# Gate and value in seven products of halves, attention jobs on a fixed plan, and a norm over all lanes

## The chip, the cores and the metric

The kernel runs on one core of a Trainium2 chip. Its time is the device time of one execution in microseconds (us); each figure is a median of several runs. The engines are called PE (matrix products; PEld is its weight load), DVE (VectorE), ACT (ScalarE) and POOL (GpSimd). SBUF is the on-chip memory that tiles lie in, its rows are called partitions; PSUM is the set of banks that PE writes its products to.

## The reference

A retention block feeds a SwiGLU block. All of the first is fp32; three of the weights are float64 in memory and are converted to fp32 on the chip.

```python
scores = (1 / sqrt(64)) * q @ k.T             # 8 batches, 8 heads, 576 tokens, 64 wide
ret = scores * gamma[h] ** (i - j)            # for i >= j, else 0
x = (ret @ v)                                 # to 4608 tokens x 512
rms = sqrt(mean(x * x, -1) + 1e-6)
xn = x / rms * rms_g
g, val = xn @ w_gate, xn @ w_val              # 512 x 1536 each
out = (g * sigmoid(g) * val) @ w_out          # 1536 x 512
```

## The kernel before

Attention is done in 32 jobs, one for each batch and pair of heads. Each works in chunks of 128 tokens and carries a state from chunk to chunk. The second block works in 12 units of 384 tokens, with features on the partitions and tokens along the columns. A unit's gate and value products are called its up phase; three output blocks of 128 tokens follow. The parts that matter here are the norm, the gate product, and the loop that decides what comes next.

```python
def norm_1(u, sq):                       # sq: squares summed over the four feature blocks
    ms = bank(f"ms_{u}")
    for s in range(NS):                  # 3 blocks of 128 tokens; tokens go to the partitions
        nc.tensor.matmul(ms[:, s : s + 1], lhsT=sq[:, 0, s * P : s * P + P], rhs=mean_w, ...)
    nc.vector.tensor_scalar(out=r, in0=ms[:, :NS], scalar1=EPS, ..., op0=ALU.add)
    nc.gpsimd.tensor_tensor(out=r, in0=r, in1=mhalf.to_broadcast([P, NS]), op=ALU.pow)   # 3 columns
    for s in range(NS):
        nc.vector.tensor_scalar(out=diag[:, s], in0=ident, scalar1=r[:, s : s + 1], ..., op0=ALU.mult)

def norm_2(u, diag):                     # ones x diag: each token's factor on all partitions
    nc.tensor.matmul(rb[:, :U], lhsT=ones, rhs=diag..., start=True, stop=True)
    for c in range(NHP):
        nc.vector.scalar_tensor_tensor(out=x[:, c], in0=x[:, c], scalar=rms_g[:, c : c + 1],
                                       in1=rb[:, :U], op0=ALU.mult, op1=ALU.mult)

def project(u, f, w, ps):                # one of 12 row blocks of gate or value
    for c in range(NHP):
        nc.tensor.matmul(ps[:, :U], lhsT=w[:, c, f * P : f * P + P], rhs=x_of[u][:, c], ...)

# (cut) the main loop: products go on until attention lags, then attention_step() runs,
# often several times in a row
due = did_a == n_attn or (did_a / n_attn - LAG) * ffn_cols > did_f * (1 - LAG)
```

## Time and profile before

| | before |
|---|---|
| time | 1504.72 us (1502.89 to 1507.06) |
| PE busy / DVE busy / POOL busy | 1336 / 390 / 176 us |
| mean clock granted to PE | 0.933 |
| first gate product | 121.4 us |
| pow on POOL | 12 times 0.87 us, over 3 columns |

An engine's busy time counts overlapping instructions once. Each digit of the page's second part is the busy share of one fortieth of the span, in tenths. The prediction below shows those lines and reads them. The one row on pow (shortest, median and longest in ns, then first and last start, and its shape):

```profile
L284 POOL TENSOR_TENSOR r<-r,mhalf x12: 850/873/878, 98.7 to 1324.3; 128x3 f32<-128x3 f32 x12
```

### The profile page before, as it was taken

What the parts mean: (1) busy time and instruction counts of PE and PEld (TensorE: products, weight loads), DVE (VectorE), ACT (ScalarE), POOL (GpSimd) and SP (SyncE); (2) the same over time, 40 slices, a digit from 0 to 9 for tenths busy, and PEclk for the clock granted to TensorE, in tenths of its full rate; (3) what the DMA queues carried; (4) which work ended last, traced back from release to release, by engine and by line L of the source; (5) the groups of instructions that cost most, each with busy time, mean ns of one, the idle gap of its engine ahead of it and who ended that gap; (6) DMA issues with size and microseconds to landing.
All of it is one profiled execution on the core that took longest, in us unless ns stands there. A gap on an engine that the chain in (4) does not pass through costs nothing.

```text
span 1503.9 us, 13309 instructions
## 1 busy us (share of the span) xinstructions
PE 1335.9 (89%) x5312; PEld 777.0 (52%) x5312; DVE 390.4 (26%) x772; ACT 160.8 (11%) x310; POOL 175.9 (12%) x212
## 2 busy tenths in 40 slices
PE   2557896999999995699999996599999999699999
PEld 2554451555655545555554554465455554455554
DVE  4786878011122114320010112431010011220010
ACT  1112221001110101110000001010000000110000
POOL 3541000011111013400000012410000000200000
PEclk9668995999999997899999998789999999699999
DMA  8664333012121025400000014520000001000000
GB/s 167 141 147 91 112 104 106 22 38 45 31 45 38 0 45 110 82 1 9 13 0 21 0 38 89 100 41 0 21 0 8 14 0 36 1 0 7 14 0 21
DMA packets 244493, 66.22 MB, mean 44 GB/s; under 512 B 225744, under 2 KB 238160, under 8 KB 244432
## 3 DMA queue, kind: packets, MB, share of 16 engines
q1 hardware_dynamic: 228928, 46.17, 14.8%
q10 hardware_dynamic: 15504, 19.21, 4.1%
q8 instruction: 42, 0.69, 0.2%
q14 instruction: 19, 0.16, 0.0%
HBM read 55.91 MB, written 9.44 MB: 43 GB/s over the span
## 4 chain that ended last, share of the span: by engine, by line
PE 83%; DVE 9%; POOL 4%; DMA 2%; issue 1%; ACT 0%; ACTq 0%; SPq 0%; DVEq 0%; POOLq 0%
PE gate L307 24%; PE val L307 24%; PE out L331 24%; PE s L174 4%; PE av L225 3%; POOL sd L212 2%; DVE ret L196 2%; PE s L184 2%; POOL qT L144 2%; DVE sum L206 1%; DVE exp L475 1%; DMA v<-in_v_dram 1%; DVE exp L472 1%; DVE exp L449 1%; DVE w_out L478 0%
## 5 line engine op out<-in xcount | busy, mean ns | idle before, releaser
L307 PE MATMUL gate<-x,w_gate 128*128 128x384 f32 x1152 | 403.7, 494 | 18.4 <-DVE x L300 17.2
L307 PE MATMUL val<-x,w_val 128*128 128x384 f32 x1152 | 397.8, 489 | 3.5 <-ACT silu L317 3.0
L331 PE MATMUL out<-w_out,h 128*128 128x512 f32 x864 | 385.5, 605 | 13.8 <-DVE w_out L478 13.8
L307 PEld LDWEIGHTS gate<-x,w_gate 128*128 128x128 f32 x1152 | 221.2, 193 | 177.0 <-issue 27.6
L307 PEld LDWEIGHTS val<-x,w_val 128*128 128x128 f32 x1152 | 219.9, 191 | 157.9 <-ACT silu L317 3.7
L331 PEld LDWEIGHTS out<-w_out,h 128*128 128x128 f32 x864 | 165.1, 193 | 225.8 <-issue 194.6
L323 DVE TENSOR_TENSOR h<-silu,val 128x384 f32<-128x384 f32 x144 | 79.8, 554 | 738.7 <-PE val L307 736.7
L212 POOL TENSOR_SCALAR sd<-sum,gc 64x256 f32<-64x256 f32 x64 | 59.9, 937 | 1007.1 <-DVE sum L206 1004.2
L174 PE MATMUL s<-qT,kT 64*128 64x128 f32 (+1 forms) x640 | 68.9, 373 | 120.5 <-POOL qT L144 104.5
L317 ACT ACTIVATE silu<-gate 128x384 f32<-128x384 f32 x144 | 70.7, 492 | 611.8 <-PE gate L307 598.7
L174 PEld LDWEIGHTS s<-qT,kT 64*128 64x128 f32 (+1 forms) x640 | 57.3, 261 | 136.6 <-POOL qT L144 107.2
L196 DVE TENSOR_TENSOR ret<-s,causal 128x768 f32<-128x768 f32 (+2 forms) x96 | 47.4, 549 | 251.8 <-PE av L225 249.3
L337 ACT COPY o<-out 128x512 f32<-128x512 f32 x36 | 21.1, 587 | 364.9 <-PE out L331 364.9
L144 POOL TENSOR_TENSOR qT<-qT,gq 128x512 f32<-128x512 f32 x64 | 54.9, 877 | 13.3 <-DVE qT L139 10.8
L225 PE MATMUL av<-ret,v 128*64 128x128 f32 (+1 forms) x640 | 54.0, 318 | 0.1
L150 POOL TENSOR_TENSOR v<-v,gv 128x512 f32<-128x512 f32 x64 | 50.4, 807 | 3.5 <-DMA v<-in_v_dram 3.5
L249 ACT COPY x<-av 128x192 f32<-128x192 f32 (+1 forms) x80 | 23.6, 357 | 238.7 <-PE av L238 231.9
L225 PEld LDWEIGHTS av<-ret,v 128*64 128x64 f32 (+1 forms) x640 | 45.3, 172 | 6.9 <-issue 6.9
L238 PE MATMUL av<-qT,sd 128*128 128x128 f32 (+1 forms) x256 | 37.1, 290 | 2.2 <-POOL sd L212 2.2
L453 ACT ACTIVATE exp<-exp,least 128x512 f32<-128x512 uint32 x36 | 26.1, 724 | 111.2 <-DVE exp L449 111.2
L238 PEld LDWEIGHTS av<-qT,sd 128*128 128x128 f32 x256 | 32.7, 200 | 4.8 <-POOL sd L212 2.3
L184 PE MATMUL s<-v,k 128*64 128x64 f32 x512 | 31.4, 291 | 0.1
(40 smaller groups left out, 372.6 us busy)
## 6 DMA issues: line engine op xcount, KB each, us to landing
qraw<-in_q_dram SPq DMA_DIRECT2D x128, 72.0 KB, 2.4
kraw<-in_k_dram SPq DMA_DIRECT2D x128, 72.0 KB, 2.5
out_dram<-o SPq DMA_DIRECT2D x36, 256.0 KB, 2.0
k<-in_k_dram SPq DMA_DIRECT2D x64, 128.0 KB, 2.5
v<-in_v_dram SPq DMA_DIRECT2D x64, 128.0 KB, 2.7
w<-in_moe_w_gate_dram ACTq DMA_DIRECT2D x12, 512.0 KB, 3.7
w<-in_moe_w_val_dram ACTq DMA_DIRECT2D x12, 512.0 KB, 4.0
w<-in_moe_w_out_dram ACTq DMA_DIRECT2D x12, 512.0 KB, 3.5
```

The lines of the kernel that those rows point to most:

```text
L144: nc.gpsimd.tensor_tensor(out=t, in0=t, in1=gq[:, hp, :n].unsqueeze(1).to_broadcast([P, m, n]), op=ALU.mult)
L150: nc.gpsimd.tensor_tensor(out=t, in0=t, in1=gv[:n, hp].unsqueeze(1).unsqueeze(3).to_broadcast([n, m, 2, D]), op=ALU.mult,)
L174: nc.tensor.matmul(d["s"][blk][:n, e, o : o + n], lhsT=d["kT"][r, ck], rhs=d["qT"][r, ck], start=True, stop=True,)
L184: nc.tensor.matmul(d["s"][1][e * D : e * D + D, 0, SC + c * D : SC + c * D + D], lhsT=d["k"][:, c, e], rhs=d["v"][:, c, e], start=True, st ...
L196: nc.vector.tensor_tensor(out=ret[:n, :, c0 * P : c0 * P + m * n].rearrange("p e (c k) -> p e c k", c=m), in0=s[blk][:n, :, o : o + m * n] ...
L212: nc.gpsimd.tensor_scalar(out=sd[j % 2][r, :, r], in0=t[r], scalar1=gc[r, hp : hp + 1], scalar2=None, op0=ALU.mult,)
L225: nc.tensor.matmul(av[blk][e * D : e * D + D, o : o + n], lhsT=d["v"][:n, c, e], rhs=d["ret"][:n, e, c * P : c * P + n], start=(c in (0, A ...
L238: nc.tensor.matmul(av[blk][:, o : o + n], lhsT=sd[j % 2][:, c - 1], rhs=d["qT"][:, c * P : c * P + n], start=False, stop=(c in (AC - 1, NC ...
L307: nc.tensor.matmul(ps[:, :U], lhsT=w[:, c, f * P : f * P + P], rhs=x_of[u][:, c], start=(c == 0), stop=(c == NHP - 1),)
L317: nc.scalar.activation(out=h_of[u, f], in_=ps[:, :U], func=AF.Silu)
L323: nc.vector.tensor_tensor(out=h, in0=h_of[u, f], in1=ps[:, :U], op=ALU.mult)
L331: nc.tensor.matmul(ps[s][:, :DM], lhsT=h_of[u, f][:, s * P : s * P + P], rhs=w_out[:, f], start=(f == 0), stop=(f == NF - 1),)
```

## The change

Its intent is fewer products: with each matrix cut in two by two blocks, Winograd's form of Strassen's scheme needs seven products of halves where the plain one needs eight, at the price of additions on DVE. Attention jobs get fixed places among the products. Work is moved off POOL, and the norm is computed for all partitions at once, so that no diagonal matrix is needed. The diff is cut to its core.

```diff
 def norm_1(u):
-    for s in range(NS):
-        nc.tensor.matmul(ms[:, s : s + 1], lhsT=sq[:, 0, s * P : s * P + P], rhs=mean_w, ...)
-    nc.vector.tensor_scalar(out=r, in0=ms[:, :NS], ..., op0=ALU.add)
-    nc.gpsimd.tensor_tensor(out=r, in0=r, in1=mhalf.to_broadcast([P, NS]), op=ALU.pow)
-    (cut: the diagonal, and its product with ones)
+    nc.tensor.matmul(ms[:, :U], lhsT=ones, rhs=t_of[u], start=True, stop=True)   # ones = 1/512
+    nc.vector.tensor_scalar(out=r, in0=ms[:, :U], ..., op0=ALU.add)
+    nc.gpsimd.tensor_tensor(out=r, in0=r, in1=mhalf.to_broadcast([P, U]), op=ALU.pow)
 (cut)
+def up(u, m, g):                      # m: gate or value; two row blocks of each half
+    product(A11, x_, True);   nc.scalar.copy(out=s1, in_=pairs_of(x_))
+    product(S2, y, True);     add(u2, s1, y)
+    product(S1, z, True);     add(u4, u2, z)
+    product(A12, x_, False);  result(f, 0, "c11", None, x_)
+    product(S3, w, True);     result(f + NH, 1, "c22", u4, w)
+    product(S4, z, False);    result(f, 1, "c12", u2, z)
+    product(A22, w, False);   result(f + NH, 0, "c21", u2, w)
 (cut: in norm_2, four sums of x on DVE; in join, four sums of weights on POOL)
-        nc.gpsimd.tensor_tensor(out=t, in0=t, in1=gq[...], op=ALU.mult)        # t: qT
+            nc.vector.tensor_tensor(out=x_of[u][...], in0=av[blk][...], in1=gq[...], op=ALU.mult)
 (cut: the scaling of v and of the state from POOL to ACT; the clamp of exponents from DVE to ACT)
+SLOTS = (((0, 2, 4, 5), 5), ((6,), 9), ((1, 3, 5), 10))   # places of jobs in units 3k, 3k+1, 3k+2
+def behind(u, i):
+    at, n = SLOTS[u % 3]
+    if i in at:
+        slot(u // 3 * 8 + n + at.index(i))
+    if u + 1 < NU and 5 <= i < 8:                          # 5: last products; 6, 7: output blocks
+        (norm_0, norm_1, norm_2)[i - 5](u + 1)
```

## The prediction

> **What bounds the kernel now.** I read the page's first two parts, then its costliest groups, then a table by stage, then the waits of TensorE (PE).
>
> ```profile
> span 1503.9 us, 13309 instructions
> PE 1335.9 (89%) x5312; PEld 777.0 (52%) x5312; DVE 390.4 (26%) x772; ACT 160.8 (11%) x310; POOL 175.9 (12%) x212
> ...
> PE   2557896999999995699999996599999999699999
> ...
> DVE  4786878011122114320010112431010011220010
> ...
> PEclk9668995999999997899999998789999999699999
> DMA  8664333012121025400000014520000001000000
> ```
>
> PE is busy 89% of the span. It is thin only in the first seven slices (37.6 us each), where DVE stands at 4 to 8 tenths, and in three dips later.
>
> ```profile
> L307 PE MATMUL gate<-x,w_gate 128*128 128x384 f32 x1152 | 403.7, 494 | 18.4 <-DVE x L300 17.2
> L307 PE MATMUL val<-x,w_val 128*128 128x384 f32 x1152 | 397.8, 489 | 3.5 <-ACT silu L317 3.0
> L331 PE MATMUL out<-w_out,h 128*128 128x512 f32 x864 | 385.5, 605 | 13.8 <-DVE w_out L478 13.8
> L323 DVE TENSOR_TENSOR h<-silu,val 128x384 f32<-128x384 f32 x144 | 79.8, 554 | 738.7 <-PE val L307 736.7
> ```
>
> An fp32 product appears as two instructions (576 gate products, 1152 rows). The mean durations overlap; the pace comes from the chain of waits:
>
> ```profile
> 722.94 2.58 PE gate L307 x8
> 784.86 30.90 PE out L331 x72
> ```
>
> Eight instructions of 384 columns take 2.58 us, 322.5 ns each; 72 of 512 take 30.90, 429.2 each. Both are 2 x columns / 2.4 + 2.5 ns. At that pace the work is gate and value 2304 x 0.3225 = 743 us, output 864 x 0.4292 = 371, 32 attention jobs x 4.2 = 134 (one warm job runs from 912.71 to 916.91), norm about 16: 1264 us. The other 240 us of the 1504 are idle time and half clock. Where, by stage:
>
> ```profile
> 0.00:121.45 121.45, 55.92 (x557) 48.59 (x557) 86.72 (x150) 16.91 (x33) 59.02 (x67) 0.77 0.72 149
> 121.45:284.00 162.55, 144.08 (x377) 74.07 (x378) 104.34 (x202) 31.80 (x49) 1.73 (x2) 0.88 0.30 92
> ...
> 912.00:992.00 80.00, 48.22 (x467) 40.07 (x466) 32.22 (x73) 7.12 (x19) 34.44 (x43) 0.74 0.54 103
> 992.00:1054.00 62.00, 62.00 (x202) 37.09 (x201) 14.95 (x31) 8.65 (x14) 1.72 (x2) 1.00 0.01 2
> ```
>
> The columns are length, then busy time of PE, PEld, DVE, ACT, POOL, then clock, DMA share, GB/s. No gate product runs before 121 us, where nine attention jobs and the conversion of float64 weights share DVE. Later, whenever attention jobs come in a burst (912 to 992), a job takes 11 us for 4.2 us of PE work, because
>
> ```profile
> PE s L174 <- POOL qT L144: 104.5, 21, 5.8
> ```
>
> GpSimd scales the state and then q between one job and the next.
>
> **What the Trainium skill says.** "TensorE: Matmul & The Clock Gate", section "Back-to-back issue gap", gives N/2.4 + 2.5 ns warm; the trace agrees if each fp32 instruction counts its columns twice. Its section "LDWEIGHTS" gives P/1.2, 107 ns for 128 columns; in the trace the carried-state products with 128 columns start 111 to 112 ns apart, and so do the mean products with one column, so about 112 ns is the floor for a stream in which each product loads new weights. "VectorE: DVE Perf Modes", section on the errata, gives (N+151)/0.96 for an fp32 tensor_tensor: 557 ns at 384; the trace has 554. "GPSIMD Engine Reference", section 3.1, puts a two-input operation at about 2.6 cycles per element; the trace's 512-column multiplies take 1103 and 1297 ns. No page gives the cost of a pow there.
>
> **The change, part by part.**
>
> *Seven products.* Per unit of 384 tokens and matrix: 7 products x 6 row blocks x 2 halves = 84 matmuls of 192 columns in place of 48 of 384. One instruction should take 2 x 192 / 2.4 + 2.5 = 162.5 ns, above the 112 ns floor, so weight loading stays hidden. 12 units x 2 x 84 x 2 = 4032 instructions x 0.1625 = 655 us, 88 less than 743. The price is on DVE: per pair of gate row blocks 5 additions out of PSUM, per pair of value blocks 5 plus 4 multiplies, 14 x 36 = 504 operations x 0.554 = 279 us in place of 80. Within a unit's up phase (336 x 0.1625 = 54.6 us of PE) that is 42 x 0.554, some 23 to 25 us: it fits. The tightest wait is the last product, which accumulates on a bank that the addition before must have read: PE has one product, 8 x 0.1625 = 1.3 us, to cover it, and DVE needs 0.27 (in the trace, end of stream to start of h) + 0.55 + about 0.1. It fits if DVE's queue is empty.
>
> *Norm.* One broadcast mean product replaces three small ones and one diagonal product: 8 us less on PE. But pow on GpSimd goes from 3 columns to 384. Three took 873 ns; a GpSimd multiply extrapolated to zero width (458 ns at 64, 1297 at 512) is 338 ns. At most 535 / 3 = 178 ns per column remain, which would be 68 us per unit; if most of it is fixed, 10 to 20 us. This is the largest unknown. Between the mean product and the next unit's first product lie two output blocks, 20.6 us, less about 4 us for DVE: pow is hidden up to some 17 us. I take 20 us at the start, where nothing hides it, and hidden afterwards.
>
> *Attention.* q's decay moves into the copy out of PSUM, v's and the state's scaling to ACT. PE no longer waits for GpSimd to finish qT, and jobs are spread singly behind products instead of in bursts. DVE per job, from the rows by form: mask about 1.4, state sum 1.05, three copies of 192 columns 1.07, transposes 1.5, 5.0 us in all, beside 4.2 us of PE work and followed by products that need DVE late. So a job should cost its 4.2 us and perhaps 1 more.
>
> *Weights.* One DVE pass (0.496 us) of six goes to ACT: 3.9 down to about 3.4 us per chunk of 36. The four sums per group are GpSimd's: about 5 us x 6, beside other work.
>
> *Sum.* Start: the first transpose comes at about 15 us as now; five jobs x 5.0 plus eight chunks x 3.4 plus two chunks begun make 54 us of DVE; norm about 9 and pow 20: the first product at about 102 us (now 121.5, after nine jobs). Unit 0's up phase carries 28 chunks (95 us of DVE), its own 24 us and four jobs (20 us): 139 us of DVE against 72 of PE. With imperfect overlap 160. Then 11 up phases x 54.6 = 601, 12 down phases x 30.9 = 371, norms 8, the 24 jobs left x 4.2 = 101, tail 4, waits 25 (1 us per job). 102 + 160 + 601 + 371 + 8 + 101 + 4 + 25 = 1372; I say 1375.
>
> **The rivals.** (a) *Pow becomes the bound.* For it: 873 ns for three columns, no figure anywhere for more, and the state's scaling has been moved off GpSimd as if to keep it free. Against it: tiny instructions are mostly fixed cost, and the norm is split into three stages with an output block between. At 40 us per unit, 23 us of each would show: about 1375 + 20 + 11 x 23 = 1650; at 68 us about 1960. I give "visibly not hidden" one chance in five. (b) *DVE becomes the bound in steady state*, through its in-order queue: a job's 5 us burst ahead of the additions makes the last product of the next pair wait. For it: DVE rises from 390 to some 640 us. Against it: 45% of the span, and the first need after a job comes 2.6 us into the next pair. Two to three us per job and one per pair would add 100 to 120 us: about 1490, near the same. (c) *Half-width matmuls lose the gain*: if the pace were 190 ns (the recorded length of a weight load) instead of 162.5, gate and value would take 766 us and the change would keep only its scheduling part: about 1480. Against it: the 112 ns floor. (d) *The weight stage hides less*: unit 0 at half clock, since PE is busy only half of it; the trace shows clock 0.5 from 233 to 264 us in the same stage. That is 30 us more at most.
>
> **Range and chances.** If pow is hidden, waits of 0 to 100 us and a start of 85 to 140 us give about 1320 to 1450. The top of the range also takes a pow of about 28 us or a moderate form of (b). Range 1315 to 1500. Below 1473 (2% faster): 0.78. Within 2%: 0.07. Slower than 1534: 0.15, nearly all from (a).
>
> **What would show it.** The product rows of 192 columns should number 4032 and run 8 in 1.30 us. The pow row is the first to look at: over 17 us, DVE's scaling of x waits for it and PE for DVE at every unit's start. PE should wait for GpSimd nowhere in attention. The first product should come near 102 us, and the first output block near 262. DVE should be busy about 640 us and be PE's main releaser only in the first 260. It would be wrong if pow is long, if the waits of PE on DVE after unit 0 exceed 60 us, or if the 192-column pace is not 162.5.

## The result, and the profile after

| | before | after |
|---|---|---|
| time | 1504.72 us | 1877.23 us (1874.94 to 1879.2) |
| ratio | 1 | 1.2474 (95% interval 1.2449 to 1.2499) |
| PE / DVE / POOL busy | 1336 / 390 / 176 us | 1229 / 605 / 773 us |
| mean clock | 0.933 | 0.832 |
| first gate product | 121.4 us | 144.9 us |

The change makes the kernel a quarter slower. The page of the changed kernel:

```profile
span 1872.9 us, 17016 instructions
PE 1228.9 (66%) x6968; PEld 979.0 (52%) x6968; DVE 605.4 (32%) x1185; ACT 298.2 (16%) x570; POOL 772.5 (41%) x42
...
PE   3207657396397399198199099199099189379199
...
POOL 0492306607506604805704802902902901923900
PEclk9657878698699699599599599699599699789599
```

PE's busy time fell as planned. But PE now has a hole every few slices, and after the first slice POOL is busy wherever PE has its hole. Only 42 instructions ran on POOL in all. Twelve of them are the costliest group on the page, and under it stand two of the new products (columns: count, busy us, mean ns of one, then idle time ahead of the group and who ended it):

```profile
L301 POOL TENSOR_TENSOR r<-r,mhalf 128x384 f32<-128x384 f32 x12 | 738.2, 61519 | 873.5 <-DVE r L300 873.5
L336 PE MATMUL x<-x,w_gate 128*128 128x192 f32 x576 | 127.1, 371 | 551.4 <-DVE x L307 537.6
...
L336 PE MATMUL w<-sums,w_val 128*128 128x192 f32 x576 | 110.9, 338 | 12.1 <-DVE c L343 12.1
```

One pow takes 61.5 us. The products of the first kind begin each unit, and have 551 us of idle time ahead of them; those of the second kind, with the tight wait of the prediction, have 12. The table of waits gives the same chain from its two ends (total us, times, longest):

```profile
DVE x L307 <- POOL r L301: 740.4, 12, 61.7
...
PE x L336 <- DVE x L307: 537.6, 12, 63.0
```

DVE waits for pow, PE waits for DVE. In order of time, for the second unit of the changed kernel (start, length):

```profile
294.42 0.81 PE L298 MATMUL ms<-sq,ones 128*128 128x384 f32 x2
...
295.90 61.54 POOL L301 TENSOR_TENSOR r<-r,mhalf 128x384 f32<-128x384 f32 x1 [63.14 <-DVE r L300]
```

```profile
311.80 4.03 PE L384 MATMUL out<-w_out,h 128*128 128x512 f32 x9
357.47 2.21 DVE L307 SCALAR_TENSOR_TENSOR x<-x,rms_g,r 128x384 f32<-128x384 f32 x4 [61.65 <-POOL r L301]
358.23 2.90 PE L336 MATMUL x<-x,w_gate 128*128 128x192 f32 x8 [42.41 <-DVE x L307]
```

The two output blocks that stand between the mean product and the next unit end at about 316 us; then PE has nothing to do for 42.4 us. All eleven gaps of this kind read 43.0 to 45.5 us from start to start of PE's products. PE's granted clock falls to half in them (0.50 from 320 to 361 us), so the next products start slowly too: the first eight of the unit above took 2.90 us, where 1.30 is the pace later.

### The profile page after: what moved, and what is told of

Read it like the earlier page. It is cut to its first block, busy times and chain, and to the rows that moved or that the text cites. A ratio compares the mean times of both kernels' runs of the same rounds, so it can differ in the third digit from the quotient of the medians.

```text
span 1872.9 us, 17016 instructions
## 1 busy us (share of the span) xinstructions
PE 1228.9 (66%) x6968; PEld 979.0 (52%) x6968; DVE 605.4 (32%) x1185; ACT 298.2 (16%) x570; POOL 772.5 (41%) x42
## 4 chain that ended last, share of the span: by engine, by line
PE 46%; POOL 36%; DVE 9%; POOLq 3%; ACT 3%; DMA 1%; issue 1%; SPq 0%; DVEq 0%; ACTq 0%
POOL r L301 36%; PE w L336 9%; PE z L336 9%; PE x L336 9%; PE out L384 8%; PE y L336 5%; POOLq L584 3%; PE s L186 2%; PE av L236 2%; DVE x L307 1%; PE av L250 1%; DVE exp L481 1%; ACT exp L458 1%; ACT exp L457 1%; ACT exp L461 1%
## 5 line engine op out<-in xcount | busy, mean ns | idle before, releaser
L301 POOL TENSOR_TENSOR r<-r,mhalf 128x384 f32<-128x384 f32 x12 | 738.2, 61519 | 873.5 <-DVE r L300 873.5
L336 PE MATMUL x<-x,w_gate 128*128 128x192 f32 x576 | 127.1, 371 | 551.4 <-DVE x L307 537.6
L336 PEld LDWEIGHTS x<-x,w_gate 128*128 128x128 f32 x576 | 111.0, 219 | 563.0 <-issue 547.5
L336 PE MATMUL w<-sums,w_val 128*128 128x192 f32 x576 | 110.9, 338 | 12.1 <-DVE c L343 12.1
L336 PE MATMUL x<-x,w_val 128*128 128x192 f32 x576 | 109.5, 334 | 8.6 <-ACT m L360 8.6
L336 PE MATMUL w<-sums,w_gate 128*128 128x192 f32 x576 | 108.9, 333 | 8.2 <-DVE h L343 8.2
L336 PE MATMUL z<-x,w_val 128*128 128x192 f32 x576 | 105.9, 327 | 2.3 <-DVE u L343 2.3
L336 PEld LDWEIGHTS w<-sums,w_val 128*128 128x128 f32 x576 | 100.4, 198 | 13.2 <-DVE c L343 13.2
L336 PE MATMUL z<-x,w_gate 128*128 128x192 f32 x576 | 105.5, 326 | 0.3 <-DVE u L343 0.3
L336 PEld LDWEIGHTS w<-sums,w_gate 128*128 128x128 f32 x576 | 98.3, 195 | 9.1 <-DVE h L343 9.1
L336 PEld LDWEIGHTS x<-x,w_val 128*128 128x128 f32 x576 | 96.1, 193 | 10.8 <-ACT m L360 10.8
```

Of the source, the lines that this page charges most:

```text
L336: nc.tensor.matmul(ps[:, i * HU : i * HU + HU], lhsT=w_up[m][:, 2 * blk + c, cut], rhs=t_of[u][blk][:, c], start=(start and i == c == 0), ...
```

## The experiments

The theory: a pow costs POOL a time per column, some 159 ns, and this alone is the loss; all the rest of the change is a gain. Nine kernels tested this, its rivals, and the other parts.

### 1. Only the norm put back (e1)

```diff
-        nc.tensor.matmul(ms[:, :U], lhsT=ones, rhs=t_of[u], start=True, stop=True)
-        nc.gpsimd.tensor_tensor(out=r, in0=r, in1=mhalf.to_broadcast([P, U]), op=ALU.pow)
+        (as before: three one-column products, pow over 3 columns, the diagonal;
+         in norm_2 its product with ones, and the scaling reads that)
```

> The changed kernel with only the norm put back as it was before: three mean products of one column, pow over 3 columns, a diagonal and one product to spread it. Theory (pow over 384 columns, 61.5 us each, is the whole loss): the 11 gaps of PE of 43 to 45.5 us between units shrink to 2 us or less, and the first product comes about 60 us earlier; 1877 - 11 x 42 - 61 + 8 = about 1360 us. Rival (DVE, with 605 us instead of 390, or half-width matmuls hold PE as well, and would take the place of pow): over 1450 us. Correct result.

Measured: 1322.26 us (1321.36 to 1324.07), correct; ratio to the kernel before 0.8784 (0.877 to 0.8799). The change with this one part undone is 12% faster than the kernel before, and 555 us faster than the change as it was. Its page:

```profile
span 1321.0 us, 17197 instructions
PE 1210.0 (92%) x7040; PEld 968.9 (73%) x7040; DVE 608.6 (46%) x1222; ACT 298.2 (23%) x570; POOL 45.0 (3%) x44
...
PE   2536556999999999999999999999999999999998
...
PEclk9658888999999999999999999999999999999999
```

After the first seven slices nothing is left to see: PE is full and its clock is 1. Two stretches follow: in the changed kernel, from one unit's first output block to the next one's first products; in this one, a whole step from a unit's first output block to the next one's (length, then busy time of PE, PEld, DVE, ACT, POOL, clock, DMA share, GB/s):

```profile
284.20:359.70 75.50, 33.09 (x80) 15.28 (x79) 7.68 (x18) 5.57 (x12) 61.54 (x1) 0.73 0.11 26
```

```profile
230.10:316.90 86.80, 86.80 (x418) 69.32 (x418) 32.40 (x66) 16.20 (x33) 0.87 (x1) 1.00 0.10 23
```

DVE has as much work as in the changed kernel (609 and 605 us), and PE waits for it nowhere after unit 0: the table of PE's waits is empty from 230 us to the end. So the rival, that DVE or the half-width products would take pow's place, falls. The 38 us by which the run beats what was expected lie in the steps: a unit lost 45.3 us (below), not the 42 put down for it, and 11 x 3.3 = 36.

The loss adds up. From the start of one unit's first output block to the next one's, the changed kernel takes 1554.2 us in eleven steps, this one 1055.9: 498.3 us, or 45.3 for each unit. The first output block starts at 284.1 and 230.1: 54 us more. Together 552, and the two spans differ by 551.9.

### 2. Pow over half the columns (e2)

```diff
-        nc.gpsimd.tensor_tensor(out=r, in0=r, in1=mhalf.to_broadcast([P, U]), op=ALU.pow)
+        nc.gpsimd.tensor_tensor(out=r[:, :HU], in0=r[:, :HU], in1=mhalf.to_broadcast([P, HU]), op=ALU.pow)
```

> The changed kernel with pow over the first 192 of the 384 columns only (a wrong result on purpose: the other columns stay unraised). Theory (pow costs GpSimd a time per column; the line through 873 ns at 3 and 61516 at 384 is 395 ns + 159 ns per column): the row reads about 31.0 us, and as nothing else fills the gap, each unit and the start save 30.5 us: 1877 - 12 x 30.5 = about 1511 us. Rival (a fixed cost of the wide form, such as a one-time or per-instruction load, or a lock between GpSimd and DVE): the row stays over 45 us and the time over 1650.

Measured: 1507.96 us (one run, state unknown), a wrong result as intended. The row, with shortest, median and longest in ns:

```profile
L301 POOL TENSOR_TENSOR r<-r,mhalf x12: 30915/30916/30935, 82.3 to 1382.8; 128x192 f32<-128x192 f32 x12
```

873 ns at 3 columns, 30916 at 192 and 61516 at 384 lie on one line to 0.2%: (61516 - 30916) / 192 = 159.4 ns per column, and 873 - 3 x 159.4 = 395 ns fixed. There is no one-time cost in it: the twelve rows lie within 20 ns of each other. The saving of 369 us is 12 x 30.8, as the line has it.

### 3. The wide pow in the kernel before (e4)

```diff
 (in the kernel before)
-        (three one-column products, pow over 3 columns, diagonal, its product with ones)
+        nc.tensor.matmul(ms[:, :U], lhsT=ones, rhs=sq[:, 0], start=True, stop=True)
+        nc.gpsimd.tensor_tensor(out=r, in0=r, in1=mhalf.to_broadcast([P, U]), op=ALU.pow)
```

> The kernel before with only the norm of the change: one broadcast mean product and pow over 384 columns. Theory (pow takes 61.5 us wherever it is, and DVE's in-order queue stops at the scaling that waits for it): each unit loses 61.5 us less the three steps between the two parts of the norm, 10 to 20 us, so 12 x 45 more, about 2000 us or more, since GpSimd also scales q there. Rival (the loss is in the new schedule, which leaves pow too little room; the old one would hide it): under 1650.

Measured: 2131.13 us (one run, state unknown), correct. The old schedule does not hide pow: it loses 626 us to it, where the new one loses 555. PE waits there for POOL's scaling of q, too:

```profile
DVE x L287 <- POOL r L280: 491.8, 9, 61.7
...
PE s L174 <- POOL qT L144: 271.9, 21, 62.7
```

The second line stood at 104.5 in the kernel before. So the new plan of jobs is not to blame.

### 4. Eight products with the narrow norm (e3)

```diff
 (e1, with)
-        (seven products of 192 columns, additions on DVE, sums of x and of weights)
+        for c in range(NHP):
+            nc.tensor.matmul(ps[:, :U], lhsT=w_up[m][:, 4 * half + c, cut], rhs=x_of[u][:, c], ...)
```

> The kernel of the first run here with gate and value as eight full products (384 columns, four per row block, no additions, no GpSimd sums), everything else as in the changed kernel. Theory (seven products are worth their PE time, 88 us over 12 units, less what unit 0 does not gain because DVE bounds it): 65 to 85 us slower than the first run, about 1430, so the new plan of attention jobs alone is still about 70 us faster than before. Rival (the additions and tighter waits give the 88 us back): within 20 us of the first run.

Measured: 1381.81 us (1381.34 to 1382.23), correct; ratio to before 0.918. So without seven products the rest of the change, with the narrow norm, is worth 1505.63 - 1381.81 = 124 us, and seven products are worth 1381.81 - 1322.26 = 59.6 us, a little under the range expected. The weights are converted at the same pace per unit in both. The traces say where the rest of the 88 us is. Starts of the first output block, and the steps from there (us; jobs in a unit's step in brackets):

| kernel | first output block | next step (0 jobs) | a later step (0) | a later step (4) |
|---|---|---|---|---|
| e1, seven products | 230.1 | 86.9 | 86.9 | 103.8 |
| e3, eight products | 197.7 | 106.8 | 94.2 | 110.9 |
| e8, eight in unit 0 alone | 215.7 | 101.8 | 86.9 | 103.8 |

In an undisturbed unit seven products save 94.2 - 86.9 = 7.3 us, which is the 88 / 12 of the prediction. Up to the first output block they cost 32.4 us, of which e3 pays back 106.8 - 94.2 = 12.6 in the next step, where it still converts weights. Together 11 x 7.3 + 12.6 - 32.4 = 60.5 us, against the 59.6 of the times.

### 5. The place of q's decay, and the spreading of jobs (e5, e6)

```diff
 (e5: e1, with)
+            nc.gpsimd.tensor_tensor(out=t, in0=t, in1=gq[...], op=ALU.mult)      # t: qT, in prepare
-            nc.vector.tensor_tensor(out=x_of[u][...], in0=av[blk][...], in1=gq[...], op=ALU.mult)
+            nc.scalar.copy(out=x_of[u][...], in_=av[blk][...])
 (e6: e1, with)
-            if i in at:
-                slot(u // 3 * 8 + n + at.index(i))
+            if i == at[-1]:
+                for k in range(len(at)):
+                    slot(u // 3 * 8 + n + k)
```

> The first run's kernel with q's decay put back on GpSimd before the scores, and the copy out of PSUM on ACT again: the plan of jobs is the new one. Theory (it is the spreading that took the wait away: a job's qT is ready long before the next job when products stand between them): only the five jobs at the start, which follow each other, pay, 0 to 4 us each, so 1322 to 1345 us. Rival (moving the decay is what took the wait of PE for GpSimd away): some 3 to 5 us for each of 32 jobs, so 1420 to 1480 us.

> The first run's kernel, but a unit's attention jobs stand together, at the place of its last one, instead of one by one; q's decay stays in the copy. Theory (spreading): each job that follows another waits for DVE's transposes and copies, 3 to 5 us, and PE's clock falls; 18 to 20 such jobs outside the start, so 1322 + 60 to 100, 1380 to 1420 us. Rival (the decay's move alone makes jobs cheap): within 25 us of the first run.

Measured: 1334.88 us (1334.33 to 1335.9) for e5 and 1418.84 us (1416.66 to 1421.8) for e6, both correct and both in the theory's range. Moving q's decay is worth 13 us, spreading the jobs 97. In e5, after the start PE waits nowhere for POOL. But the theory's reason for e5's loss doesn't hold: of 12 us only 1.9 lie before the first output block, though PE waits there 22.4 us for qT, and 10.8 lie in the later steps, where the only waits of PE left are 9.1 us (14 times) for ACT, which copies out of PSUM again. In e6, from 250 us on, PE waits 47.4 us (14 times) for DVE's transposes before a job that follows another. Its first output block starts at 251.8, 22 us later than e1's; the steps after it take 74 us more, which is those waits and 25 us of longer PE busy time (1112 against 1087), at a mean clock of 0.97 against 1.00. The two parts were changed together and look like one; it is the spreading that took away the wait for qT.

### 6. Relief for DVE in unit 0 (e7)

```diff
 (e1, with)
-            nc.vector.scalar_tensor_tensor(out=dst, in0=dst, scalar=2.0**-20, in1=exp..., op0=ALU.mult, op1=ALU.mult)
+            nc.gpsimd.tensor_tensor(out=dst, in0=dst, in1=exp..., op=ALU.mult)
-    least = cell("least", -896.0)
+    least = cell("least", -916.0)
```

> The first run's kernel with the last DVE step of the weight conversion (36 times about 0.7 us) given to the idle GpSimd as a plain multiply, its 2^-20 taken into the exponent. Theory (DVE bounds the first unit, between 88 and 216 us of the first run, with 8 tenths busy): 28 of the chunks lie there, 20 us less of DVE, so 12 to 22 us faster than the first run, about 1305 us. Rival (the chain of waits between ACT, DVE and PE bounds it, not DVE's work): within 6 us of the first run.

Measured: 1319.21 us (1317.48 to 1319.44), correct: 3 us faster, not 12 to 22. DVE lost the 26 rows of that step that lay between 91 and 222 us in e1, 19 us in all, and yet was busy longer there:

```profile
91.00:222.00 131.00, 82.04 (x518) 74.69 (x516) 111.92 (x205) 69.38 (x110) 22.57 (x16) 0.84 0.50 127
```

```profile
91.00:222.00 131.00, 86.63 (x532) 78.63 (x534) 117.36 (x188) 71.23 (x112) 59.40 (x43) 0.81 0.50 127
```

The first line is e1, the second e7; the third group of figures is DVE, the fifth POOL. The rows of DVE in e7 in order of time, and then those of POOL, show why:

```profile
142.19 0.42 DVE L490 TENSOR_SCALAR w_gate<-w_out 128x512 uint32<-128x512 uint32 x1
142.65 0.69 DVE L494 SCALAR_TENSOR_TENSOR w_gate<-w_out,w_gate 128x512 f32<-128x512 uint32 x1
...
144.40 1.50 DVE L490 TENSOR_SCALAR w_val<-w_out 128x512 uint32<-128x512 uint32 x1
145.93 1.65 DVE L494 SCALAR_TENSOR_TENSOR w_val<-w_out,w_val 128x512 f32<-128x512 uint32 x1
...
150.57 0.54 DVE L359 TENSOR_TENSOR h<-u,w 128x384 f32<-128x384 f32 x1
```

```profile
144.23 1.38 POOL L505 TENSOR_TENSOR w_gate<-w_gate,exp 128x512 f32<-128x512 f32 x1 [1.94 <-DVE exp L497]
145.69 6.09 POOL L515 TENSOR_TENSOR w_gate<-w_gate 128x512 f32<-128x512 f32 x4
```

While POOL runs, the same DVE operation takes 1.50 us instead of 0.42, or 1.65 instead of 0.69. The addition that has an operand in PSUM keeps its 0.54. These two slow ones end 0.3 to 0.4 us after a POOL operation does, as if they had waited for it (145.90 after 145.61; 147.58 after about 147.2, the first of the four in the 6.09 us row). "GPSIMD Engine Reference" of the Trainium skill, section "Specifications", says that POOL's SBUF interfaces are shared with VectorE, with contention for instructions in a 2-port mode or with two SBUF inputs; the trace agrees, though it doesn't name an instruction's mode, and adds the size, about 1 us for each of these. So the miss is explained: what DVE gave away came back as longer operations. The rival's figure came true, but its reason isn't shown: what is shown is the contention, which neither side had named.

### 7. Eight products in unit 0 alone (e8)

```diff
 (e1, with)
+        if u == 0:
+            (the eight full products of e3)
+            return
 (the sums of weights on POOL come after unit 0's products)
```

> The first run's kernel with eight full products in unit 0 alone, where DVE is the bound, and seven in the other eleven units; GpSimd makes the sums of weights after unit 0's products. The first output block came at 230.1 us with seven products and at 197.7 with eight, and a later unit without attention jobs takes 86.9 us with seven against 94.2 with eight. Theory (seven products lose in unit 0 what their additions and the sums cost DVE there, and gain 7 us in each later unit): first output block near 198, then about 13 us lost in the second unit, where the rest of the conversion goes on, so about 1303 us, 1295 to 1310. Rival (GpSimd's sums, 24 of about 1.4 us, now slow DVE's conversion during unit 0's output blocks and hold up unit 1): 1318 or more.

Measured: 1322.96 us (1321.44 to 1324.02), correct: no gain, as the rival had it, though by another way. It was run on another chip. The first output block came at 215.7, not 198. POOL did most of the sums within unit 0 after all, as soon as PE had used the weights (29.8 us of POOL between 91 and 198 us); that they made the 18 us is likely after e7, but not shown. That gave 14.4 us against e1, and the second unit's step gave 14.9 back (101.8 against 86.9): PE waits in it 5.0 us for the last weights of the output product and 4.3 for the norm's squares, and its mean clock is 0.93 where e1 has 1.00. What unit 0 won was lost again in the next step.

### 8. The sums of weights on DVE (e9)

```diff
 (e1, with)
-                nc.gpsimd.tensor_tensor(out=o, in0=a, in1=b, op=op)
+                nc.vector.tensor_tensor(out=o, in0=a, in1=b, op=op)
```

> The first run's kernel with the 24 sums of weights (512 columns) on DVE instead of GpSimd. Theory (while GpSimd runs such an operation, DVE's operations with only SBUF operands take about 1 us longer each, as in the run before last 0.41 us became 1.2 to 1.5 and 0.69 became 1.64 to 1.7, so a sum of 1.4 us there costs DVE about 1 us, against 0.69 us if DVE does it itself): 24 x 0.3 = 7 us less, so 1312 to 1319 us. Rival (the two engines do not hinder each other; DVE only gets 24 x 0.69 = 17 us more work in the stage that it bounds): 1332 to 1340 us.

Measured: 1326.94 us (1326.07 to 1327.51), correct: 4.7 us slower than e1, between the two ranges. This run was on another chip, where the kernel before took 2.2 us more, and the two ratios to it (0.8806 and 0.8784) have overlapping intervals; the traces are clearer. The first gate product comes at 92.2 us against 89.7 and the first output block at 234.3 against 230.1, so 2.5 us were lost in the start and 1.7 in unit 0; all later steps are alike. DVE's busy time rose by 5.2 us (613.8 against 608.6), though it took over 16.6 us of sums. So the contention is real, but it cost DVE only 11.4 / 24 = 0.5 us for each sum on POOL, not the 1 us that I took.

## Why the prediction was wrong

The prediction gave 1375 us, range 1315 to 1500, and 0.78 for faster; 1877 was measured. By its own steps:

- **Norm: the step that failed.** "If most of it is fixed, 10 to 20 us", and "I take 20 us at the start, where nothing hides it, and hidden afterwards". The row read 61.5 us, each of the twelve times. The bound of 178 ns per column that the prediction had worked out, 68 us, was near the truth; most of the 0.87 us that three columns took beyond a small instruction was per column (159 of the 178 ns), not fixed. The two arguments against the rival, that tiny instructions are mostly fixed cost and that the norm was split into three stages (as if fitted to pow's length), were guesses and not readings.
- **Its slack was right.** The prediction put 17 us of room beside pow. 61.5 - 17 = 44.5 us per unit; 45.3 were lost. Its own rival (a) with the measured pow in it, 1375 - 20 + 61.5 + 11 x 44.5, is 1906 us, and 1877 was measured; the rest of the sum was too high (last point). (Its own figure for 68 us, about 1960, leaves the 20 us at the start; with 68 there, too, the sum is 1984.) So the mechanism stood in the document; the choice between 20 and 68 us was made wrong, and could not be made from one duration.
- **Seven products: right.** 4032 rows of 192 columns start 162 to 163 ns apart in the median, so weights stay hidden; an undisturbed unit is 7.3 us shorter, 88 / 12. The whole gain is 60 us, not 88: 32 us are lost up to the first output block, where the weights are converted too, and 13 come back. That the conversion is the reason is argued and not shown; e7 to e9 moved its work about and gained 3 us at most. The rivals (b) and (c), DVE in steady state and a pace of 190 ns, are ruled out by e1. Of (d), half clock in unit 0, nothing was lost against the estimate: its up phase took 140 us in e1, at a mean clock of 0.83.
- **DVE's work: right in size.** 605 us measured, 640 predicted.
- **Attention: right in time, partly wrong in cause.** A job costs 4.2 us of PE: in e1 a unit with four jobs takes 103.8 - 86.9 = 16.9 us more. The "perhaps 1 more" of waiting did not come. The prediction named the move of q's decay and the spreading together; e5 and e6 give 13 and 97 us.
- **The sum without pow.** 1372 - 20 = 1352 predicted; e1, which has the norm's 8 us of products back, took 1322. The differences are the first product at 89.7 instead of 82 us, unit 0's up phase 140 instead of 160 us, and about none of the 25 us of waits: 1352 + 8 + 8 - 20 - 25 = 1323. (The start's terms, 15 + 54 + 9 + 20, make 98 us and not the 102 that the prediction took.)

## What to carry to other kernels

A duration measured at one small size bounds a cost from above and says nothing of how it grows: where the change goes to a hundred times that size, the upper bound has to be taken for the estimate, or the size measured first. When a part of a change is slow, put that part back alone: here the rest was worth 12%. And work given to an idle engine isn't free where it shares SBUF interfaces with a busy one: e7 moved 19 us of work from DVE to POOL, and DVE was busy 5 us longer.

## What the Trainium skill lacked or had wrong

- "GPSIMD Engine Reference" has no cost for pow (nor has any other page): 395 ns + 159.4 ns per column of 128 partitions in fp32, from 873, 30916 and 61516 ns at 3, 192 and 384 columns. Its 2.6 cycles per element for two-input operations in section 3.1 (an estimate of 2.2 ns at the page's 1.2 GHz) must not be carried over to pow.
- The same page names the contention of POOL and DVE in section "Specifications" without a size ("SBUF — State Buffer", section "Terms", describes it as a lock held for a whole instruction, so the skill as a whole lacks the durations only). Behind a POOL multiply or sum of 512 columns, DVE's TENSOR_SCALAR went from 0.42 to 1.50 us and its SCALAR_TENSOR_TENSOR from 0.69 to 1.65; operations with a PSUM operand kept 0.54 to 0.55.
- "TensorE: Matmul & The Clock Gate", section "Back-to-back issue gap", leaves out fp32, for which "FP8 and Floating Point Precision", section "TensorE Precision Notes", counts four passes without a time. Here each fp32 product is two instructions, and each takes 2N/2.4 + 2.5 ns warm: 162 to 163, 322.5 and 429.2 ns at 192, 384 and 512 columns. Section "LDWEIGHTS" gives 107 ns for 128 columns; the norm's fp32 products of one column, each with a load of 128 columns, started 112 ns apart in the median.
